# Window attention on one core: the first x in quarters, a key shift from half the keys, and ScalarE evicting at the end

## The chip, the cores and the metric

The kernel runs on one core of a Trainium2 chip. The metric is the device time of one execution in microseconds. A core has five engines that run their own instruction streams and meet at semaphores: TensorE (PE in the profile, its weight loads PEld) multiplies matrices from SBUF into PSUM, VectorE (DVE), ScalarE (ACT) and GpSimd (POOL) work elementwise, SyncE (SP) here only issues DMAs. PSUM has eight banks of 128 x 512 float32. ScalarE and GpSimd can issue DMAs too, in order with their other work.

## The reference: two window attentions and a projection

x is 224 x 224 tokens of 96 channels in bf16. The first 48 channels of q, k, v attend within horizontal bands of 8 rows, the last 48 within vertical bands of 8 columns; each of the 2 x 28 bands has 1792 tokens.

```python
qkv = einsum('bhwc,cd->bhwd', x, wqkv)
ah = softmax(einsum('bqc,bkc->bqk', qh, kh) * scale, axis=-1)   # 28 bands of 1792 tokens, 48 channels
oh = einsum('bqk,bkc->bqc', ah, vh)
...                                                             # the same for the vertical bands
o = concat(oh, ov)
return einsum('bhwc,cd->bhwd', o, wo)
```

A softmax doesn't change when the same vector is taken off every key. The kernel uses that: it shifts the keys by a mean key, to keep the scores small.

## The kernel before

Two bands that lie side by side make a pair; there are 28 pairs P, 14 horizontal and then 14 vertical. Both bands of a pair are worked on at once, in two halves of the 128 partitions. For each pair TensorE makes K, Q (transposed) and V from the turned x; then come 4 chunks of queries (512, 512, 512, 256) against 14 tiles of 128 keys. A score tile covers 2 PSUM banks, 128 x 1024. Most score tiles go to ScalarE, which takes the exponential in one instruction (`emit_qk`, line 867; banks 0, 1 and 2, 3 in turn). The others (246 tiles) get an exponential from a polynomial on VectorE and GpSimd (lines 989 to 1006). PV products (line 723) gather each chunk with its row sum; VectorE evicts it to `OT_sb` (line 884). Horizontal results are turned and kept in `oh_all`. In the vertical phase the two halves are joined, projected with wo (`out_fills`, line 644, called g), evicted to `og` (line 650) and stored. For the last pair the vertical half is projected on its own (`fin_fills`, line 611, called f) and added to `og` with a reciprocal of the sum (lines 618 and 623), two stores' worth of rows at a time.

The whole program is unrolled at build time. `Sched` keeps each engine's list of instructions and derives the semaphore waits from the keys that an instruction reads and writes. The order of the middle comes from `ORDER`, 28 strings, one a pair: `q` is a score tile for ScalarE, `1` to `4` the two score products of a polynomial tile (`3`, `4` and, in capitals, `K`, `G` take two neighbouring banks), `v` a PV product, `k` a K, Q or V product of the next pair, `g` and `f` the output products. A planner in the same file walks the string, keeps a planned time for each engine (`tm`), and uses it to order VectorE's and GpSimd's work and to choose the queue of a store. Constants at the top of the file are its durations; `XR1` and `XR2` are the planned times at which the turned x of pairs 1 and 2 is there. Score products of tiles 1 to `NTWICE` are issued twice.

Ahead of the first string stands a written-out head. The first pair's x comes as two halves for each band, four DMAs, on SP's and ScalarE's queues, then wqkv on SP's; behind these SP blocks, loads and turns the x of pair 1 (lines 291 and 408). TensorE spins on a tile of zeros (`spin`, line 372) until x is there, then transposes it: 8 groups of 4 transposes (`t_lead`, line 745), each group evicted to `xT_sb` by VectorE (line 757) or ScalarE (line 761) with a running sum into `xs_sb`. From all 8 sums a small product (`KB`, line 767) makes the shift `kb_sb` (line 771). Q[0] and K[0] are the first 512 queries and keys; Q[0] is evicted by ScalarE (line 547), K[0] by VectorE with the shift added (line 778), its first 128 keys apart from the rest. Spinning products fill TensorE's planned idle time, in `lead_pe` ahead of each product, and after K[0]'s eviction up to its planned end. `emit` writes every engine's list in that order, so an instruction that waits holds back all that stands behind it on its engine.

At the end `store` gives each finished piece of output to SP's, ScalarE's or GpSimd's queue by planned times.

Of the kernel before, what the change touches and what calls it, by code (L numbers as in the profile page):

```python
# [32 lines left out]
D_ST, D_SW, D_TAIL = 1.0, 0.60, 1.0  # L33
XR1, XR2, TURN = 19.5, 43.0, 4.5
# [5 lines left out]
NTWICE = 11  # L40
# [5 lines left out]
    "kkqqkkq3q3q3qkqkqkqkq1q1qvvq4qkvqkv4qkqvv1qkvqvqvvq4vqkvvqkvq1vqvvq1vkqvkq4vqkvq1vqv2qvkqkqvkq2vvq3qvvvqvkq2vqvvkq",  # L46
    "1qvvvqvq2vvq1qvvqvvq3vvqvvqvkqkvqvKqvvq4qvkvq2qvvq2vqv1qvvqvqv1qvvvq4qvkvq3qvkq2vqv2qvq3vqkvqvvqkq4vqvvq4vqkvq3vqkvvqk",
    "v2qvqv1qvvvvq1qvvvvqvq3vvqvq3kqqvvqvkq4vkqq2vkqv1qkvqvvq4qvkvq3qkvqvkq2qvvq4vqkvq1vvq2qvvkq2qvv1qvvqvvqkvqvvkq1vqv2qvvq",
    "1vq2qvvq1vvqvqvvvqv1qvq1vvqvqvq4qkvq1vqvvqvq2vqv1qvv4qkqvv1qvqvkq2vqkvvq2vkqvkq3vqkqvvvqv1qvq4vqkq3vqkvq4vqvkvq4vqkvq2vk",
    "qvq1vvqvvqv2qvq1vq2qvvvqv2qvvq1qvvvqvvq1qvvqvkvqvkq1qvkqvkvq4vqvvq1qv2qkvqkv1qvvqkvqq2vqkvq1qkvvq2qvvvq1qkkqvvq2vkqvv1",  # L50
    "qvqvvqv2qvvq1vvqvv1qvvqvqv2qq4vqvkq1vqvvvqvq1vqkvkqkvvq2kqv3qkvqv4qvvqkq1vqvvvqkqvv4qvqkv2qvvq2vqv1qvq4vqvvqkvkvq1qkvvq2v",
    "vq1qvvqvvq1vvqvq1vqvvqvv3qvvqvvqvkq2qv1qvqkv2qkvqvq2vvq1qkvvvq2kqq4vqvkq1vvqkqvvq4qkvqv1qvq4vkqvq3vkqvvq3qkvqvvqvvkvq",
    "2qvv1qvvq2vq3qvvqvvqvvq1vqvvvqkqvkvq1qvvkqv2qkvqv2qkvvq1vqv4qvkqvvq2vq4qvvkq1qvkvqvvqv2qvvq2qvv3qvkqv1qvvqkvq4vqvkvq4qvvvkq1",
    "qvvqvvq2vvqvvq1vq2qvvvq1qvvqvq1vkqvvqvkqvkqv2qkvqv2qkq1vqvvq2vqv2qvkvqkq1vqv1qvqvvvqv1qkqvvvq1qkvq2qvkqv2qvvvq1kqvvqk",
    "vqvvq2vvq4qvvvvq1vqvvq4qvkq1qvvqvvvq2vqv1qvvqvkqvkqvvvq2q1qvvq1vvqkvq2vkqv3qkvqvvqvqkq4vqkq3vqvvq4vqkvqk2qvvq1vqvvkq2qkv",
    "vq1vvqvqvvvqv2qvvq1vqvkqkvkqv4qvqvk1qkqvvqv2qvq1vkqvqvvvqv4qvqkq3vqkvq3vqvvq4vqkvq2vqv1qvvqkqvvvqv3qkvqv2qvq1vkqvq2vqv2",
    "qvv1qvqvvvqvv2qvq1vvq1qvvqv1qvqvvq3qvvqvkkqkvq4qkvqv4qkvqv2qvvqv2qvvq3vqvkq1qvvqvkq4qvkqv1qvvvq2qkvqv1qvv2qvkqvkvq2qvk",
# [117 lines left out]
def bass_standalone__window_attn_cswin__vision_kernel(  # L175
# [28 lines left out]
    with es:  # L204
# [1107 lines left out]
        def do_fill(c):  # L1312
# [28 lines left out]
            if g == ("Q", 0, NCH - 1):  # L1341
                turn_x(2)
# [109 lines left out]
```

## Time and profile before

| | us |
|---|---|
| three runs | 1055.43, 1056.22, 1056.88 |
| median of them | 1056.22 |
| the profiled execution | 1057.54 |
| its span, first to last instruction | 1055.7 |
| ScalarE busy in the span | 1041.8 |
| TensorE, VectorE, GpSimd busy | 1027.3, 1014.0, 985.1 |

In a row of the profile a group has its line, engine, operation, the tile written and the tiles read, shapes, the count, the busy time and the mean of one in ns, and then the idle time of the engine ahead of it with what ended it. In a row of the order of time the first number is the start in us from the span's start, the second the length of the merged group; a group's members can overlap, as matmuls do. A row of stages has the stretch, its length, the busy time with the count, the granted TensorE clock, the share of DMA and GB/s.

### The profile page before, as it was taken

To read this page: it belongs to the slowest core of one execution; us is meant where nothing else is said; L and a number is where in the kernel's file an instruction comes from. 1 tells how busy PE (TensorE), PEld (TensorE's weight loads), DVE (VectorE), ACT (ScalarE), POOL (GpSimd) and SP (SyncE) were. 2 spreads that over 40 slices of the span, in tenths; PEclk is the share of its full clock that TensorE was granted. 3 is DMA by queue.
4 is the path that set the end of the run, shared out by engine and by line. 5 is a ranking of instruction groups with operands and counts; after the bars stand their busy time and mean duration, and the time that the engine had idled before them with its cause. 6 is when DMAs were issued, how large, how long until landed. Compare 5 with 4: busy or idle time off the path is not lost.

```text
span 1055.7 us, 32757 instructions
## 1 busy us (share of the span) xinstructions
PE 1027.3 (97%) x13456; PEld 385.9 (37%) x13456; DVE 1014.0 (96%) x1748; ACT 1041.8 (99%) x1137; POOL 985.1 (93%) x654
## 2 busy tenths in 40 slices
PE   9999999999999999999999999999999999999998
PEld 4333333333333333333333433434333333333343
DVE  7989999999999999999999999999999999999998
ACT  7999999999999999999999999999999999999997
POOL 7999999999988998999999999988999999999997
PEclk9999999999999999999999999999999999999999
DMA  9867527654752854222176545537634553674352
GB/s 191 171 133 140 102 51 145 112 96 89 141 94 56 143 104 74 36 59 55 30 77 92 81 91 101 92 52 109 96 64 82 88 91 67 101 100 52 66 75 69
DMA packets 413079, 96.84 MB, mean 92 GB/s; under 512 B 403648, under 2 KB 410016, under 8 KB 412928
## 3 DMA queue, kind: packets, MB, share of 16 engines
q1 hardware_dynamic: 412080, 93.66, 51.8%
q8 instruction: 105, 1.72, 0.7%
q0 software_dynamic: 448, 0.69, 0.2%
q10 hardware_dynamic: 400, 0.39, 0.1%
q14 instruction: 46, 0.38, 0.1%
HBM read 28.31 MB, written 28.21 MB: 54 GB/s over the span
## 4 chain that ended last, share of the span: by engine, by line
PE 54%; ACT 22%; DVE 10%; POOL 7%; issue 6%; DMA 0%; ACTq 0%; POOLq 0%; DVEq 0%
ACT PT L867 22%; PE ps L723 20%; PE ps L697 20%; PE ps L710 7%; DVE PT L994 3%; POOL PT L1002 3%; PE ps L530 3%; DVE qb L989 3%; POOL PT L1005 2%; PE ps L575 1%; POOL PT L1006 1%; PE ps L644 1%; DVE PT L991 1%; DVE og L650 1%; DVE V_sb L582 1%
## 5 line engine op out<-in xcount | busy, mean ns | idle before, releaser
L867 ACT ACTIVATE PT<-ps 128x1024 bf16<-128x1024 f32 x1126 | 1037.2, 1080 | 4.1 <-PE ps L697 2.9
L1002 POOL TENSOR_TENSOR PT<-PT 128x1024 f16<-128x1024 f16 x246 | 461.8, 1894 | 20.3 <-DVE PT L991 11.3
L697 PE MATMUL ps<-QT_sb,KT_sb 49*64 49x512 bf16 (+1 forms) x5332 | 461.6, 362 | 15.9 <-ACT PT L867 9.7
L723 PE MATMUL ps<-PT,V_sb 128*49 128x512 bf16 (+1 forms) x3136 | 464.4, 361 | 0.0
L994 DVE SCALAR_TENSOR_TENSOR PT<-ps,PT 128x512 uint16<-128x512 f32 (+1 forms) x405 | 312.4, 799 | 15.7 <-PE ps L710 6.8
L989 DVE TENSOR_SCALAR qb<-ps 128x512 f16<-128x512 int16 (+1 forms) x421 | 313.7, 775 | 11.9 <-PE ps L710 7.8
L1005 POOL TENSOR_TENSOR PT<-qb 128x1024 f16<-128x1024 f16 x150 | 283.2, 1894 | 22.9 <-DVE qb L989 10.8
L697 PEld LDWEIGHTS ps<-QT_sb,KT_sb 49*64 49x64 bf16 x5332 | 135.4, 104 | 308.3 <-ACT PT L867 284.2
L723 PEld LDWEIGHTS ps<-PT,V_sb 128*49 128x49 bf16 x3136 | 134.2, 103 | 205.7 <-issue 173.5
L710 PE MATMUL ps<-QT_sb,KT_sb 50*64 50x512 bf16 (+1 forms) x1968 | 196.6, 390 | 5.3 <-DVE PT L994 1.2
L1006 POOL TENSOR_SCALAR PT<-PT 128x1024 f16<-128x1024 f16 x150 | 156.9, 1046 | 12.8
L991 DVE SCALAR_TENSOR_TENSOR PT<-ps,qb 128x512 f16<-128x512 int16 (+1 forms) x172 | 123.0, 743 | 0.2
L710 PEld LDWEIGHTS ps<-QT_sb,KT_sb 50*64 50x64 bf16 (+1 forms) x1968 | 55.8, 103 | 76.3 <-DVE PT L994 22.9
L884 DVE CAST OT_sb<-ps 113x512 bf16<-113x512 f32 x112 | 68.9, 615 | 0.5 <-PE ps L723 0.4
L544 DVE CAST QT_sb<-ps 128x512 bf16<-128x512 f32 (+1 forms) x111 | 67.0, 614 | 1.7 <-PE ps L530 1.0
L535 DVE TENSOR_SCALAR_CACHE_REDUCE KT_sb<-ps 128x512 bf16<-128x512 f32 x106 | 63.8, 617 | 1.3 <-PE ps L530 0.8
L650 DVE CAST og<-ps 128x480 bf16<-128x480 f32 x84 | 51.4, 617 | 1.4 <-PE ps L644 0.7
L582 DVE CAST V_sb<-ps 128x480 bf16<-128x480 f32 (+1 forms) x84 | 51.3, 616 | 0.4 <-PE ps L575 0.4
L530 PE MATMUL ps<-xT_sb,w_sb 97*64 97x512 bf16 x224 | 41.9, 371 | 0.3 <-DVE qb L989 0.2
L530 PE MATMUL ps<-xT_sb,wq_sb 97*64 97x512 bf16 x224 | 40.8, 367 | 0.1
L575 PEld LDWEIGHTS ps<-w_sb,xT_sb 96*64 96x64 bf16 x1568 | 33.5, 112 | 16.1 <-issue 7.1
L575 PE MATMUL ps<-w_sb,xT_sb 96*64 96x48 bf16 x1568 | 39.1, 190 | 0.0
(66 smaller groups left out, 248.6 us busy)
## 6 DMA issues: line engine op xcount, KB each, us to landing
xT_sb<-xt_dram SPq DMA_DIRECT2D x28, 336.0 KB, 5.2
xp_dram<-in_x_dram SPq DMA_DIRECT2D x26, 336.0 KB
oc_all<-xp_dram SPq DMA_DIRECT2D x26, 336.0 KB, 3.6
xt_dram<-xT_sb SPq DMA_DIRECT2D x26, 336.0 KB, 6.5
out_dram<-og SPq DMA_DIRECT2D x181, 48.0 KB, 2.0
oh_all<-ohn SPq DMA_DIRECT2D x52, 84.0 KB, 2.8
stg<-oh_all SPq DMA_DIRECT2D x13, 336.0 KB, 6.0
xt_dram<-xT_sb SPq DMA_DIRECT2D x4, 168.0 KB, 4.6
```

The lines of the kernel that those rows point to most:

```text
L530: ins = e.matmul(bk[64 * w:64 * w + 64, 0:qs], lhsT=lw, rhs=xT_sb[b][0:C + 1, w, q0:q0 + qs], start=True, stop=True)
L575: ins = e.matmul(bk[64 * h:64 * h + 64, j * C2:(j + 1) * C2], lhsT=xT_sb[b][0:C, w, t0:t0 + 64], rhs=w_sb[0:C, wblk(P, "v"), 0:C2], start= ...
L697: ins = e.matmul(bank(SETS[s] + w)[64 * kh:64 * kh + 64, i * t["qs"]:(i + 1) * t["qs"]], lhsT=KT_sb[b][64 * w:64 * w + CA, kt * 128 + 64 * ...
L710: ins = e.matmul(bank(bp[w])[64 * kh:64 * kh + 64, 0:512], lhsT=KT_sb[b][64 * w:64 * w + nr, kt * 128 + 64 * kh:kt * 128 + 64 * kh + 64], ...
L723: ins = e.matmul(bank(pb)[64 * w:64 * w + CA, 0:t["qs"]], lhsT=V_sb[b][:, w, kt, :], rhs=PT[slot][:, ca:ca + t["qs"]], start=st and i == 0 ...
L867: S.commit("act", 0.0, D_ACT, None, lambda e, s=s, slot=slot: e.activation(PT[slot][:], ps[:, 512 * SETS[s]:512 * SETS[s] + 1024], ACTF.Ex ...
L989: fn, reads, writes = lambda e: e.tensor_scalar(q, l, m, a, ALU.mult, ALU.add), bk, qk
L991: fn, reads, writes = lambda e: e.scalar_tensor_tensor(y.bitcast(FP16), l, -RA * 2.0 ** 16, q, ALU.add, ALU.mult), bk + qk, ptk
L994: fn, reads, writes = lambda e: e.scalar_tensor_tensor(y.bitcast(U16), f, 128.0, y.bitcast(FP16), ALU.mult, ALU.add), bk + ptk, ptk
L1002: square = ("pool", D_SQ, lambda e: e.tensor_tensor(y, y, y, ALU.mult), yk + ["pser"], yk)
L1005: return [("pool", D_SQ, lambda e: e.tensor_tensor(y, q, q, ALU.mult), qk, yk), ("pool", D_AF, lambda e: e.tensor_scalar(y, y, -(QS * (RB ...
L1006: ("pool", D_AF, lambda e: e.tensor_scalar(y, y, -(QS * (RB + RA) / 2) ** 2, 1.0, ALU.add, ALU.mult), yk + ["pser"], yk),
```

## The change

Five things change together.

- The first x is loaded as eight quarters in place of four halves: for each half and band one quarter on SP's queue and one on ScalarE's. wqkv keeps its place as SP's third DMA. Each group of transposes waits for its own quarter.
- The key shift is made from the sums of the first half alone, four sums in place of eight, with the factor doubled. The evictions of the second half take no sum.
- In the head the last band's second half (two groups of transposes) moves behind Q[0], KB and K[0]; KB moves ahead of K[0]; the spinning products at the head's end go. The new order begins with two score tiles, where the old one began with two K products. Score tiles are issued twice from tile 3 on, before from tile 1; the planner counts more for products while TensorE is planned to be slow.
- From the point where all score tiles are issued, ScalarE evicts the g outputs, and it evicts the last PV chunk. The planned price of a store's issue on SP or ScalarE at the end falls from 1.0 to 0.60, and a store goes to ScalarE's queue only once all PV chunks are closed.
- All 28 strings of `ORDER` are new, and the planner's start times with them.

```diff
-D_ST, D_SW, D_TAIL = 1.0, 0.60, 1.0
-XR1, XR2, TURN = 19.5, 43.0, 4.5
+D_ST, D_SW, D_END = 1.0, 0.60, 0.60
+XR1, XR2, TURN = 20.05, 43.5, 4.5
...
-NTWICE = 11
+NTW0, NTWICE = 3, 11
+CT = 9.5
...
-    "kkqqkkq3q3q3qkqkqkqkq1q1qvvq4qkvqkv4qkqvv1qkvqvqvvq4vqkvvqkvq1vqvvq1vkqvkq4vqkvq1vqv2qvkqkqvkq2vvq3qvvvqvkq2vqvvkq",
+    "qqkkqkkq1qkq3qkqkk3q1qqvq1qkqvv2qvqkvkvq2qkvqkvq3qvkvqvqvkq2kvq1qvkqkq1qvvvqkqvkq1vvq2qvvvq4qvkvq4vqkvq3vqvvvq4qkvvvq1",
...
-    "qvvv1qvvq2vqv1qvvqvvvqgvqv1qvgqgvvq1qvvvgq2qvvq2vqv1qvvvqvvqvq4vqgvq4vqvgvq3fqvvvq4vfqvvq3vqvvqvvqvgq4vfqvvq2vfqvqgvgqffqvvvfqfqfvvfqfvvvgvvfff",
+    "qvv1qvvq1qvvvqvvqv1qgvqv2qvvvq1vqv2qvvq2vqv1qvvqgvvqvqvgqv1qvvfqv2qvvq2vvq2qvvvffqvqv3qvvfqvvqvvq4vfqvvq2vqvffqvvvfqgqvvfqfvgqvgvvffvgff",
...
-        xs_sb = sb("xs_sb", [C, 2, 4], BF16)
-        kbj = sb("kbj", [128, 4], FP32)
+        xs_sb = sb("xs_sb", [C, 2, 2], BF16)
+        kbj = sb("kbj", [128, 2], FP32)
...
+        FQ = FTH // 2
         for hf in range(2):
-            for w, q in ((0, "sp"), (1, "actq")):
-                dma(q, [], [("x", w, hf)], x0_sb[:, w, hf * FTH:(hf + 1) * FTH, :],
-                    x_lead[w][:, hf * FTH * C:(hf + 1) * FTH * C], f"x{w}{hf}", land=3.4 + 1.0 * hf + 0.3 * w)
-        dma("sp", [], ["wst"], wst[:, :], wqkv, "w0", land=5.2)
+            for w in range(2):
+                for h2, q in ((0, "sp"), (1, "actq")):
+                    k0 = hf * FTH + h2 * FQ
+                    dma(q, [], [("x", w, hf, h2)], x0_sb[:, w, k0:k0 + FQ, :],
+                        x_lead[w][:, k0 * C:(k0 + FQ) * C], f"x{w}{hf}{h2}", land=3.2 + 1.9 * hf + 0.4 * w + 0.2 * h2)
+            if hf == 0:
+                dma("sp", [], ["wst"], wst[:, :], wqkv, "w0", land=4.8)
...
+                def da(e, bk, k0=k0, n=n):
+                    return e.activation(rows[:, k0:k0 + n, :], bk[:, 0:n * C].rearrange("p (s c) -> p s c", s=n), ACTF.Copy)
...
             def d(e, bk):
                 dst, src = views(bk)
+                if hf:
+                    return e.tensor_scalar(dst, src, 1.0, None, ALU.mult)
                 return e.tensor_scalar(dst, src, 1.0, None, ALU.mult, ALU.add, accum_out=acc)
...
-            return e.tensor_scalar(kbj[:, :], bk[:, 0:4], -alpha / NTOK, None, ALU.mult, ALU.add, accum_out=kb_sb[:, :])
+            return e.tensor_scalar(kbj[:, :], bk[:, 0:2], -2.0 * alpha / NTOK, None, ALU.mult, ALU.add, accum_out=kb_sb[:, :])
...
-        for w, hf, bs in ((0, 0, (6, 7)), (1, 0, (2, 3)), (0, 1, (6, 7)), (1, 1, (2, 3))):
+        for w, hf, bs in ((0, 0, (6, 7)), (1, 0, (2, 3)), (0, 1, (6, 7))):
             for h2 in range(2):
                 f = t_lead(w, hf, h2)
                 lead_pe(f, bs[h2])
                 lead_ev(f, bs[h2], 0, h2 == 1)
         flags.add(("QB", 0))
         lead_pe(Q[0], 5)
+        lead_pe(KB, 0)
         lead_pe(K[0], 4)
         lead_ev(Q[0], 5, 0, True)
-        lead_pe(KB, 0)
         lead_ev(KB, 0)
         lead_ev(K[0], 4, 0)
         lead_ev(K[0], 4, 1)
-        spin(S.done[("dve", S.cnt["dve"] - 1)])
-        spin(S.done[("dve", S.cnt["dve"] - 1)], 128)
+        for h2 in range(2):
+            f = t_lead(1, 1, h2)
+            lead_pe(f, 6 + h2)
+            lead_ev(f, 6 + h2, 0, h2 == 0)
...
                     if ia[0] >= len(act_seq):
+                        d_t = D_END
+                    if pv_open[0] >= len(pv_chunks):
                         tm["aq"] = max(tm["aq"], tm["act"])
...
+                if (P, c) == (NP - 1, NCH - 1):
+                    tm["act"] = max(tm["act"], st + L_PV) + 0.41
...
+                    S.commit("act", 0.0, 0.41, 0.51, lambda e, b0=acc[0]: e.activation(
+                        OT_sb[P % 2][0:64 + CA, q0:q0 + qs], bank(b0)[0:64 + CA, 0:qs], ACTF.Copy),
+                        [("bank", acc[0])], [("OT", P % 2, c)])
...
+            if c == "g" and ia[0] >= len(act_seq):
+                z = f["chain"][0]
+                tm["act"] = max(tm["act"], st + d + L_FILL) + z[6]
+                done = tm["act"] + 0.1
+                S.commit("act", 0.0, z[6], z[6] + 0.1, lambda e, fn=z[4], bk=bank(b[0]): fn(e, bk), [("bank", b[0])] + z[2], z[3])
+                store(z, done)
+                release(b[0], done)
+                return
```

More of the change, by code (lines that the diff above doesn't have):

```diff
@@ L263, in bass_standalone__window_attn_cswin__vision_kernel @@
             for w in range(2):
-                SEMS[f"x{b}{w}"] = sem(f"s_x{b}{w}")
+                for z in range(2):
+                    SEMS[f"x{b}{w}{z}"] = sem(f"s_x{b}{w}{z}")
                 SEMS[f"xp{b}{w}"] = sem(f"s_xp{b}{w}")
@@ L747, in t_lead @@
             n = FTH * TH
[L748 removed]
+            acc = xs_sb[0:C, w, h2:h2 + 1]
             def views(bk):
@@ L1232, in do_q @@
             st = pe_start("A", r)
-            tw = D_MM if 1 <= ia[0] <= NTWICE else 0
+            tw = D_MM if NTW0 <= ia[0] <= NTWICE else 0
+            if st < CT:
+                tw = 2 * tw + D_MM
             tm["pe"] = st + D_MM + tw
@@ L1337, in do_fill @@
             st = pe_start(f["mode"], max(r, t))
+            if c == "k" and P == 0 and st < CT:
+                d *= 2
             tm["pe"] = st + d
```

93 lines of the change are left out of this document (52 added, 41 removed).

## The prediction

> **What bounds the kernel now.** I read the page first: its line of engine times, then its costliest groups.
>
> ```profile
> span 1055.7 us, 32757 instructions
> PE 1027.3 (97%) x13456; PEld 385.9 (37%) x13456; DVE 1014.0 (96%) x1748; ACT 1041.8 (99%) x1137; POOL 985.1 (93%) x654
> L867 ACT ACTIVATE PT<-ps 128x1024 bf16<-128x1024 f32 x1126 | 1037.2, 1080 | 4.1 <-PE ps L697 2.9
> ```
>
> ScalarE is 99% busy, nearly all of it in 1126 exponentials of line 867, which the change leaves in number and shape. So I cut the span at the first and the last of them (busy time by stages, line 867 alone), and looked at ScalarE's order of time at the start.
>
> ```profile
> 0.00:10.72 10.72, 0.00 (x0) 1.00 0.75 198
> 10.72:1049.82 1039.10, 1037.20 (x1126) 1.00 0.53 91
> 1049.82:1055.71 5.89, 0.00 (x0) 0.93 0.26 77
> ...
> 10.72 5.60 ACT L867 ACTIVATE PT<-ps 128x1024 bf16<-128x1024 f32 x6 [2.26 <-PE ps L697]
> ```
>
> Three stages: a head of 10.72 us without an exponential, 1039.10 us of them, a tail of 5.89 us. The last row gives the step between two that are fed in time: (5.60 - 1.08)/5 = 0.904 us, with 1.08 the mean of one. At that step 1126 would take 1125 x 0.904 + 1.08 = 1018.1 us; 21.0 us of the middle are exponentials that start late by fractions of a microsecond. The change touches all three: it may shorten head and tail, and it rewrites the whole order that feeds the middle.
>
> **The head.** The chain of work before the first exponential, from the order of time, and who lands when:
>
> ```profile
> 0.75 0.92 ACTq L291 DMA_DIRECT2D oh_all<-in_x_dram  x2
> 1.70 1.28 ACT L330 ACT_TABLE_LOAD   x1 [1.70 <-PEq L1437]
> 4.04 3.22 PE L745 MATMUL ps<-ident,oh_all 112*96 112x112 bf16 x32 [0.37 <-DMA oh_all<-in_x_dram]
> L745 PE MATMUL ps<-ident,oh_all x32: 300/301/329, 4.0 to 7.0; 112*96 112x112 bf16 x32
> 5.05 0.54 ACT L761 ACTIVATE xT_sb<-ps 96x448 bf16<-96x448 bf16 x1 [1.85 <-PE ps L745]
> 5.97 0.59 POOL L339 COPY wq_sb<-wst 96x96 bf16<-96x96 bf16 x2
> 7.19 0.64 PE L530 MATMUL ps<-xT_sb,wq_sb 97*64 97x512 bf16 x2
> 7.62 0.64 PE L530 MATMUL ps<-xT_sb,w_sb 97*64 97x512 bf16 x2
> 7.87 0.60 ACT L547 ACTIVATE QT_sb<-ps 128x512 bf16<-128x512 f32 x1
> 8.07 0.29 PE L767 MATMUL ps<-xs_sb,w_sb 96*64 96x4 bf16 x2
> 8.22 0.62 PE L372 MATMUL ps<-warm 128*64 128x512 bf16 x1
> 8.44 0.16 DVE L771 TENSOR_SCALAR_CACHE_REDUCE kbj<-ps 128x4 f32<-128x4 f32 x1 [0.89 <-PE ps L372]
> 8.64 0.88 DVE L778 TENSOR_SCALAR KT_sb<-ps,kb_sb 128x128 bf16<-128x128 f32 x2
> 9.06 0.31 PE L372 MATMUL ps<-warm 128*64 128x128 bf16 x1
> 9.16 1.06 PE L530 MATMUL ps<-xT_sb,w_sb 97*64 97x512 bf16 x2
> 10.15 0.94 PE L697 MATMUL ps<-QT_sb,KT_sb 49*64 49x512 bf16 x12
> ```
>
> x lands at 4.04; 32 transposes, Q0, K0 and the shift follow on TensorE; then spinning products (line 372), K1 and K2 (9.16), and only then, at 10.15, the first scores, 0.57 us before the exponential. The change does three things here.
>
> First load: quarters instead of halves. How fast x moves is a row of the DMA view for 2.5 to 3.5 us:
>
> ```profile
> DMA packets 264, 0.36 MB, mean 356 GB/s; under 512 B 32, under 2 KB 264, under 8 KB 264
> ```
>
> The first transposes wait for 2 x 168 KB that share this rate, 0.97 us; with quarters for 0.48 us of it, if half a packet takes half the time, and for as long as now, if a packet costs the same at any size. Ends: 0.48 and 0 us sooner, and the second halves up to 0.5 us later. I take 0.3, nearer the byte rate: start at 3.74. [...] Behind the two added issues of each queue stand: on ScalarE the table load, 2 x 0.46 later, ending near 3.9; ScalarE idles 1.85 us before its first eviction (5.05, in future about 4.75), so it is covered, and would cost up to 0.9 else. On SP wqkv keeps its third place, now behind 168 KB instead of 336, and the next pair's blocking, loading and turning come about 0.9 us later. Its turned x is issued from 9.67 and first used at 23.43:
>
> ```profile
> 9.67 5.07 SPq L408 DMA_TRANSPOSE xT_sb<-oc_all  x2
> ...
> DMA to landing us min/median/max: 5.3/5.3/5.4
> ...
> 23.43 0.23 PE L504 MATMUL ps<-ident,wq_sb 96*64 96x96 bf16 x2 [0.22 <-DVE PT L994]
> ```
>
> Two turns share the 5.07 us of issue, so the second lands before 14.74 + 5.4 = 20.1 (and after 15.0); 0.9 later, and with the use 2 us sooner, it is 21.0 against 21.4 at the very worst. Nothing, with a stall of at most 1 us if a load in front of it is slow.
>
> Then the order. The starts of 32 transposes lie 31 steps apart, (7.0 - 4.04)/31 = 0.095 us each, 0.38 for four. Six groups of four instead of eight stand before Q0, with three short spins among them (128 columns, a quarter of the 0.43 that 512 take from 7.19 to 7.62): 3.74 + 6 x 0.38 + 0.3 = 6.3. Q0 and K0 take 0.43 each, the shift 0.15 between them (8.07 to the next product at 8.22): K0 issued at 6.88, TensorE free at 7.31; the last two transpose groups 0.76: 8.07. The spins at 8.1 to 9.2 are removed and K1, K2 go behind two score tiles, so the first scores start here if their inputs are there. VectorE: K0's product ends 6.88 + 0.64 = 7.52, the first 128 keys' eviction (0.88 for two) near 7.9. ScalarE: QT at 6.3 + 0.64 + 0.60, by 7.6, then the moved eviction of a transpose, 7.95 + 0.54 = 8.5: it stands ahead of the first exponential, which waits for it and is not delayed by it, since the scores end at 8.07 + 0.6. First exponential at about 8.7, **2.0 us sooner**. Ends: 1.3 (quarters late) and 2.4.
>
> What is late next is the clock. Products of 512 columns took, by line 530 at 7 to 10.3 us and line 697 at 12 to 15:
>
> ```profile
> L530 PE MATMUL ps<-xT_sb,w_sb x6: 634/634/636, 7.6 to 9.6; 97*64 97x512 bf16 x6
> L697 PE MATMUL ps<-QT_sb,KT_sb x32: 376/388/400, 11.8 to 14.8; 49*64 49x512 bf16 x32
> ...
> 12.71 0.63 PE L697 MATMUL ps<-QT_sb,KT_sb 49*64 49x512 bf16 x8
> ```
>
> The clock column reads 1.00 in both stretches, but TensorE runs half as fast, 0.43 a step against 0.63 - 0.39 = 0.24 (eight in two groups, 12.71), until some time after 10, when the first scores stand; I take 10.4, 3.2 us after the unbroken run of products began at 7.19. Now the kernel's first scores fall into the slow time. Up to the third tile that fits the 0.904 step. From the fourth on scores are issued twice (0.86 slow), and a V product or an extra score tile of 0.43 stands between two: 1.29 against 0.904, 0.4 us lost per exponential. If 3.2 us count from 6.3, full speed comes at 9.5, before the fourth tile (11.1): 0.1. If they count from 8.07, at 11.3: 0.5. If a further 2.5 us pass: 1.8. I take **0.5 us lost**. [...]
>
> **The tail.** The order of time after the last exponential, by engine:
>
> ```profile
> 1048.75 1.06 ACT L867 ACTIVATE PT<-ps 128x1024 bf16<-128x1024 f32 x1
> 1049.81 0.44 DVE L650 CAST og<-ps 128x288 bf16<-128x288 f32 x1
> 1050.31 0.42 DVE L884 CAST OT_sb<-ps 113x256 bf16<-113x256 f32 x1
> 1050.79 0.29 PE L611 MATMUL ps<-wov,OT_sb 49*64 49x97 bf16 x8 [0.32 <-DVE OT_sb L884]
> 1051.20 0.30 DVE L623 SCALAR_TENSOR_TENSOR og<-ps,rc,og 128x96 bf16<-128x96 f32 x1
> 1051.41 0.16 DVE L618 RECIPROCAL rc<-ps 128x2 f32<-128x2 f32 x1
> 1051.49 0.97 DVE L623 SCALAR_TENSOR_TENSOR og<-ps,rc,og 128x96 bf16<-128x96 f32 x4
> 1052.53 1.09 POOL L291 DMA_DIRECT2D out_dram<-og  x2 [0.19 <-DVE og L623]
> ...
> DMA to landing us min/median/max: 1.8/2.0/2.3
> ```
>
> The last OT eviction moves to ScalarE: 0.41 by the plan for VectorE's 0.42, no gain in itself. The output evictions go there too, behind it on an engine without exponentials by then, and VectorE loses 0.44 us and one earlier sum (0.30) from its last run: 0.3 us sooner, unless the last sums wait for ScalarE's second eviction, which ends some 0.9 us behind the last product, before the sums start. The last two stores now stand in one queue, POOL's, 1.09 us together; SP's and ScalarE's price in the plan falls from 1.0 to 0.6, so they go to two queues: one issue, 0.55, off the end, less the up to 0.5 by which those land later (1.8 to 2.3). I take 0.3 for that. **Tail 0.6 us shorter**; ends 0.1 and 0.9.
>
> **The middle.** The order lists give TensorE's items; between two scores (q) stand up to five others. Counted in the two lists: three or more items between scores 289 times before (250 of three, 38 of four, 1 of five), 305 after (262, 39, 4). A score and three items are four steps of 0.24, 0.96 us, over the 0.904, so these are where scores come late. If all 21.0 us of lateness sat there it would be 0.073 each, 16 more 1.2 us; if none did, 0; the few of five cost most, and there are three more. I take **1.0 us lost**. As every row of the list differs, the lateness may scatter by 1.5 us either way about that.
>
> **Sum.** -2.0 + 0.5 - 0.6 + 1.0 = -1.1 us. The profiled execution took 1057.54 us, 1.84 outside its span, and stands 1.32 over the median of the three runs, 1056.22. I put the sum on the median: **1055.1 us**, 0.1% less. A difference under 0.2%, 2.1 us, is about what a measurement of this kernel can't tell from no change.
>
> **The rivals.** (a) The middle costs nothing or gains, and the clock rises early: -2.0 - 0.6 + 0.1 with a middle of -0.3, -2.8: 1053.4 us. For it: head and tail are worked from single rows, and the middle's count is a weak guide. Against: it needs two costs to vanish. Chance 0.30.
>
> (b) The quarters come no sooner and the second ones 0.4 us later: a head gain of 1.4 in place of 2.0, 1055.7 us. For it: twice the packets at one rate. Against: first transposes need half the bytes. Chance 0.09.
>
> (c) TensorE stays slow to about 13.8, three or four exponentials lose 0.43 each beyond the 0.5: 1.3 us more, 1056.4 us. For it: transposes interrupt the run of products at 7.3 to 8.1. Against: the products are nearly unbroken from 6.3. Chance 0.13. [...]
>
> (d) Slower: the new list feeds the exponentials worse. Place: scores behind three or more items, in all 28 pairs; price: lateness of 21.0 us grows. Head, clock and tail leave 1056.22 - 2.1 = 1054.1, so it decides from 4.2 us more lateness on, a fifth: 1058.3. At 5 us more it is 1059.1 us. For it: no row of the old list stands, and the old places say nothing of the new. Against: only 6% more places of the long kind. Chance 0.10.
>
> **The numbers.** The forecast has 0.38, with (b) and (c) 0.60 for within 0.2%; (a) 0.30 faster; (d) 0.10 slower. The forecast's own range is 1054.1 to 1056.5; the one given reaches to (a)'s gain with a better middle, 1052.4, and towards (d), 1057.8.
>
> **What would show it.** Right: first transpose near 3.7, first exponential near 8.7, products at 634 ns until 10 to 11.5, last stores on two queues, 5.3 us behind the last exponential; the middle longer than 1039.1 by 0 to 3 us. Wrong: a first exponential behind 9.4, a wait of TensorE for x between transposes, scores 0.4 us late beyond the sixth exponential, or a middle of over 1043.

## The result: 15% slower, and what the profile after shows

The changed kernel takes 1215.1 us in the median (six executions, 1208.0 to 1219.5), the kernel before 1056.0 us beside it (six, 1055.4 to 1056.9). The ratio is 1.1506, 95% interval 1.1469 to 1.1544. The forecast was 1055.1 us, so 160 us are to be explained. The profiled execution took 1213.5 us.

From the page of the changed kernel:

```profile
span 1211.7 us, 32739 instructions
PE 1080.8 (89%) x13448; PEld 392.9 (32%) x13448; DVE 1017.4 (84%) x1739; ACT 1052.2 (87%) x1138; POOL 983.7 (81%) x650
...
PEclk9897999889799889989999999798999889798999
...
L882 ACT ACTIVATE PT<-ps 128x1024 bf16<-128x1024 f32 x1126 | 1046.8, 1071 | 152.3 <-PE ps L706 128.2
...
L536 PE MATMUL ps<-xT_sb,wq_sb 97*64 97x512 bf16 x224 | 43.2, 380 | 105.8 <-DMA xT_sb<-xt_dram 58.7
```

ScalarE does nearly the same work as before (1052.2 us busy against 1041.8, again 1126 exponentials), but it sat idle 152.3 us ahead of the exponentials, line 882 now, where it was 4.1. They waited for scores. TensorE itself is busy 53.5 us longer, and its clock row has many slices of 7 and 8. The last row is the odd one: ahead of the Q products (`wq_sb`; K products read `w_sb`) TensorE sat idle 105.8 us, waiting for DMAs into `xT_sb`. The same group before the change, and then the part of it in the changed kernel that has 256 columns:

```profile
L530 PE MATMUL ps<-xT_sb,wq_sb 97*64 97x512 bf16 x224 | 40.8, 367 | 0.1
...
L536 PE MATMUL ps<-xT_sb,wq_sb 97*64 97x256 bf16 x56 | 9.8, 341 | 101.8 <-DMA xT_sb<-xt_dram 58.7 <-DMA xT_sb<-oc_all 43.1
```

A Q product of 256 columns is the fourth and last chunk of a pair, and nearly all of the waiting is ahead of these. The three stages, cut at the exponentials as in the prediction:

```profile
0.00:7.79 7.79, 0.00 (x0) 1.00 0.65 181
7.79:1206.78 1198.99, 1046.81 (x1126) 0.92 0.44 79
1206.78:1211.73 4.95, 0.00 (x0) 0.72 0.48 129
```

Head and tail came out shorter, as forecast: 7.79 against 10.72 and 4.95 against 5.89. All the loss is in the middle, 1199.0 against 1039.1. The view of waits of the changed kernel (total us, times, longest) says who waits for whom there:

```profile
ACT PT L882 <- PE ps L706: 128.2, 79, 14.8
DVE QT_sb L550 <- PE ps L536: 102.9, 19, 13.3
...
PE ps L536 <- DMA xT_sb<-xt_dram: 58.7, 9, 9.3
PE ps L536 <- DMA xT_sb<-oc_all: 47.0, 8, 13.8
```

Line 550 evicts Q products, so it is a Q product each time. The kernel before has no wait of TensorE for `xT_sb` in that view. The longest case, in the order of time (SyncE's queue and TensorE):

```profile
44.41 2.76 SPq L293 DMA_DIRECT2D xt_dram<-xT_sb  x1
...
44.88 0.41 PE L706 MATMUL ps<-QT_sb,KT_sb 49*64 49x512 bf16 x4
...
47.22 3.39 SPq L293 DMA_DIRECT2D xp_dram<-in_x_dram  x2
...
50.65 0.55 SPq L293 DMA_DIRECT2D wo<-in_wo_dram  x1
51.26 0.87 SPq L293 DMA_DIRECT2D wov<-in_wo_dram  x2
52.17 1.33 SPq L293 DMA_DIRECT2D wov<-one_sb  x2
...
53.61 3.14 SPq L414 DMA_TRANSPOSE xT_sb<-oc_all  x2
...
59.11 0.43 PE L536 MATMUL ps<-xT_sb,wq_sb 97*64 97x256 bf16 x2 [13.82 <-DMA xT_sb<-oc_all]
...
60.74 0.64 PE L706 MATMUL ps<-QT_sb,KT_sb 49*64 49x512 bf16 x4
```

TensorE stops at 45.3 and stands still for 13.82 us in front of a Q product of 256 columns, a last chunk. It waits for a turned x that SyncE starts only at 53.61, behind a store, a blocking and the loads of wo. That x cannot be the product's own: the pair's K and first Q products were made from their x long before.

The code says whose x it is. `xT_sb` has two buffers, so pair P and pair P + 2 share one. At the first score tile of a pair, `do_q` calls `queue_prep`, which commits the refill of that pair's buffer with the x of the pair two further on (`turn_x`, later `plan_x`). Instructions that are committed behind it see the new contents. In the old order every Q product of a pair stands ahead of the pair's first `q`. In the new one 20 do not: the last chunk's product of the 19 pairs 1, 2, 5 to 7, 9 to 14, 18, 19 and 22 to 27, and one more of pair 5, stand one or two `q` behind it. For pairs 26 and 27 there is no pair two further on and so no refill, and their late products, at 1132.21 and 1169.34, wait for nothing. The other 18 read the refilled buffer: Q of those queries is made from the x of the pair two further on, which is also a wrong result. They make 17 waits, since the two of pair 5 share one, and 17 is what the last two rows of the view of waits count. The order can be read off the strings. A pair's share of `q` is 41 for pair 0, and the old first string has 41; the new first string has 43, the last 39, and all between are out of step by two. The new first string ends in

```
q4qkvvvq1
```

and its 42nd `q`, the second from its end, is pair 1's first score tile; the `k` behind it is pair 1's last Q product.

What follows the waits costs time too. Busy time by stretches (PE, PEld, DVE, ACT, POOL, then the granted clock, DMA share and GB/s):

```profile
45.00:59.00 14.00, 0.28 (x4) 0.00 (x0) 1.23 (x1) 1.68 (x2) 12.34 (x23) 0.62 0.89 186
59.00:65.50 6.50, 6.39 (x40) 1.74 (x40) 2.91 (x5) 3.06 (x4) 1.07 (x1) 0.50 1.04 179
66.00:80.00 14.00, 13.69 (x156) 4.75 (x152) 12.26 (x22) 13.76 (x16) 7.04 (x5) 1.00 0.36 86
```

After the wait TensorE is full (6.39 of 6.50 us), but at half clock, and ScalarE gets work for 3.06 us of the 6.5. From 66 on the clock is back and ScalarE is full again. In the clock record 16 stretches at half clock lie between the head and the tail, 188 us together, some of it inside the waits; only the wait of 2.12 us at 613.02 has none behind it.

A ledger of the middle, from the starts of the 1126 exponentials in order of time, each distance less a step of 0.908 us: 18 of them come more than 1.5 us late, 115.8 us together, and 17 of these 18 are one behind each of the 17 waits; 67 more come 0.2 to 1.5 us late inside a stretch at half clock or within 2 us behind it, 44.8 us. That is 160.6 us, and the middle grew by 159.9. What is left, about 16 us, is what the kernel before has in all (16.5).

### The profile page after: what moved, and what is told of

It is laid out like the page before. It is cut to its first block, busy times and chain, and to the rows that moved or that the text cites. A ratio compares the mean times of both kernels' runs of the same rounds, so it can differ in the third digit from the quotient of the medians.

```text
span 1211.7 us, 32739 instructions
## 1 busy us (share of the span) xinstructions
PE 1080.8 (89%) x13448; PEld 392.9 (32%) x13448; DVE 1017.4 (84%) x1739; ACT 1052.2 (87%) x1138; POOL 983.7 (81%) x650
## 4 chain that ended last, share of the span: by engine, by line
PE 52%; ACT 18%; DMA 7%; DVE 7%; POOL 6%; issue 5%; SPq 4%; ACTq 0%; DVEq 0%; POOLq 0%
PE ps L732 21%; PE ps L706 19%; ACT PT L882 18%; PE ps L719 7%; SPq L293 4%; DMA xT_sb<-xt_dram 4%; DMA xT_sb<-oc_all 3%; PE ps L536 3%; DVE qb L1009 3%; POOL PT L1022 2%; POOL PT L1025 2%; DVE PT L1014 1%; PE ps L581 1%; PE ps L650 1%; POOL PT L1026 1%
## 5 line engine op out<-in xcount | busy, mean ns | idle before, releaser
L882 ACT ACTIVATE PT<-ps 128x1024 bf16<-128x1024 f32 x1126 | 1046.8, 1071 | 152.3 <-PE ps L706 128.2
L706 PE MATMUL ps<-QT_sb,KT_sb 49*64 49x512 bf16 (+1 forms) x5324 | 479.9, 377 | 14.6 <-ACT PT L882 9.6
L732 PE MATMUL ps<-PT,V_sb 128*49 128x512 bf16 (+1 forms) x3136 | 492.4, 382 | 0.4 <-DVE KT_sb L939 0.2
L1009 DVE TENSOR_SCALAR qb<-ps 128x512 f16<-128x512 int16 (+1 forms) x424 | 314.8, 771 | 41.7 <-PE ps L719 37.8
L706 PEld LDWEIGHTS ps<-QT_sb,KT_sb 49*64 49x64 bf16 x5324 | 138.3, 105 | 310.5 <-ACT PT L882 253.4
L732 PEld LDWEIGHTS ps<-PT,V_sb 128*49 128x49 bf16 x3136 | 141.0, 106 | 232.1 <-issue 190.9
L719 PE MATMUL ps<-QT_sb,KT_sb 50*64 50x512 bf16 (+1 forms) x1968 | 206.2, 409 | 4.2 <-DVE PT L1014 1.1
L1026 POOL TENSOR_SCALAR PT<-PT 128x1024 f16<-128x1024 f16 x150 | 156.5, 1043 | 12.7
L536 PE MATMUL ps<-xT_sb,wq_sb 97*64 97x512 bf16 x224 | 43.2, 380 | 105.8 <-DMA xT_sb<-xt_dram 58.7
L899 DVE CAST OT_sb<-ps 113x512 bf16<-113x512 f32 x111 | 68.7, 618 | 8.8 <-PE ps L732 8.4
L536 PEld LDWEIGHTS ps<-xT_sb,wq_sb 97*64 97x64 bf16 x224 | 13.2, 110 | 121.7 <-issue 92.7
L986 POOL TENSOR_TENSOR stg<-OT_tr,rn 128x768 bf16<-128x768 bf16 (+1 forms) x26 | 34.1, 1312 | 9.7 <-PE ps L732 5.7
```

The lines of the kernel that those rows point to most:

```text
L536: ins = e.matmul(bk[64 * w:64 * w + 64, 0:qs], lhsT=lw, rhs=xT_sb[b][0:C + 1, w, q0:q0 + qs], start=True, stop=True)
L706: ins = e.matmul(bank(SETS[s] + w)[64 * kh:64 * kh + 64, i * t["qs"]:(i + 1) * t["qs"]], lhsT=KT_sb[b][64 * w:64 * w + CA, kt * 128 + 64 * ...
L719: ins = e.matmul(bank(bp[w])[64 * kh:64 * kh + 64, 0:512], lhsT=KT_sb[b][64 * w:64 * w + nr, kt * 128 + 64 * kh:kt * 128 + 64 * kh + 64], ...
L732: ins = e.matmul(bank(pb)[64 * w:64 * w + CA, 0:t["qs"]], lhsT=V_sb[b][:, w, kt, :], rhs=PT[slot][:, ca:ca + t["qs"]], start=st and i == 0 ...
L882: S.commit("act", 0.0, D_ACT, None, lambda e, s=s, slot=slot: e.activation(PT[slot][:], ps[:, 512 * SETS[s]:512 * SETS[s] + 1024], ACTF.Ex ...
L899: S.commit("dve", 0.0, 0.6, 0.75, lambda e: e.tensor_copy(OT_sb[P % 2][0:64 + CA, q0:q0 + qs], bank(pb)[0:64 + CA, 0:qs]), [("bank", pb)], ...
```

## The experiments

**Do the late products make the loss?** Theory: the late Q products, through the refill, are the loss. The expectations count 20 waits, one for each late product; the traces have 17, as said above. Rival 1 is that the quarters hold up SP's queue; rival 2 is that the new order feeds the exponentials worse throughout, as rival (d) of the prediction has it. Two kernels take the dependence away in different manners, and a third gives it to the old order.

The first pulls each late product ahead of its pair's first score tile.

```diff
+        owed = 0
         for c in "".join(ORDER):
+            while c == "q" and begun and act_seq[ia[0]]["P"] not in begun and prep_q:
+                do_fill("k")
+                owed += 1
+            if c == "k" and owed:
+                owed -= 1
+                continue
```

> The changed kernel, but every Q product that stands behind the first score tile of its own pair in the new order (20 of them, in 19 pairs) is issued just ahead of that tile; nothing else is moved. Theory: each of these 20 waits for the refill of the x buffer that the first tile of the pair has queued, TensorE stands idle behind it, and the clock falls. Then the time is that of my blind sum, 1052 to 1057 us, with no wait of TensorE for x and no slow stretch of the clock between 15 and 1050 us. Rival 1, the quarters hold up SP's queue and every turned x is late: the waits stay, over 1150. Rival 2, the new order is uneven as a whole or too thin at the start to hold the clock: over 1150 too.

Measured: 1070.1 us (six executions, 1069.8 to 1070.4 and one of 1080.8), ratio 1.0147 (1.0119 to 1.0176). No product behind the head waits for x, and the clock record stays at full speed from 6.34 us to 1067.89. So 145 of the 160 us are gone. The forecast for this run was missed: its middle is 1055.4, 16.3 over that of before, and about half of the extra shows at the handovers. Where products were pulled up in front of a pair's first score, the exponentials come up to 1.0 us late (at 194.2, 268.5, 455.4 and others): the first six exponentials of each of these 19 pairs come 10.3 us late all together, and 2.1 in the kernel before. Where the other half lies was not traced.

The second leaves the order as it is and queues the refill only once the last Q product of the pair has been issued.

```diff
+        held = []
+        def refill():
+            P = held[0]
+            if any(f["gives"][:2] == ("Q", P - 1) for f in prep_q):
+                return
+            held.pop(0)
...
         def queue_prep(P):
...
-            if 2 <= P < NPH - 1:
-                turn_x(P + 1)
...
+            held.append(P)
```

> The changed kernel with its order of scores and products untouched; instead the DMAs that refill the x buffer of the pair just begun are queued only when the last Q product of that pair has been issued. The late products then read their own pair's x again (in the changed kernel they read the x of the pair two further on). Theory: what costs is only the dependence on the refill, so 1052 to 1060 us. Rival 2, the place of the products in TensorE's order costs by itself: over 1150. Rival 1: over 1150.

Measured: 1054.7 us (ten executions: six from 1054.3 to 1054.8, four from 1065.1 to 1065.4), ratio 1.0028 (0.9999 to 1.0057). From its trace, the three stages, the stretch that stood still in the changed kernel, and the group that waited:

```profile
0.00:7.99 7.99, 0.00 (x0) 1.00 0.63 179
7.99:1047.83 1039.84, 1037.45 (x1126) 1.00 0.52 91
1047.83:1052.78 4.94, 0.00 (x0) 1.00 0.48 129
```

```profile
45.00:59.00 14.00, 13.80 (x152) 4.93 (x152) 12.22 (x18) 14.00 (x17) 12.75 (x24) 1.00 0.86 182
```

```profile
L536 PE MATMUL ps<-xT_sb,wq_sb 97*64 97x512 bf16 x224 | 41.2, 364 | 0.4 <-DVE QT_sb L550 0.2 <-DVE wq_sb L567 0.2
```

The same items in the same order, and 105.8 us of idle time are 0.4. The middle is 1039.84, 0.75 us over before. That settles the main question: this order as an order costs next to nothing, what it does to the refill costs 160 us. The four executions near 1065 are a matter of their own, taken up below.

The third is the kernel before, with the last Q product of those 19 pairs held back to just behind the pair's first score tile.

```diff
+        late, due = {1, 2, 5, 6, 7, 9, 10, 11, 12, 13, 14, 18, 19, 22, 23, 24, 25, 26, 27}, False
         for c in "".join(ORDER):
+            if c == "k" and prep_q[0]["gives"][0] == "Q" and prep_q[0]["gives"][2] == NCH - 1 and prep_q[0]["gives"][1] in late:
+                due = True
+                continue
             if c == "q":
                 do_q()
+                if due and act_seq[ia[0] - 1]["P"] == prep_q[0]["gives"][1]:
+                    do_fill("k")
+                    due = False
```

> The kernel before with one thing changed: in the same 19 pairs the last Q product (256 queries) is moved behind the pair's first score tile; head, tail, loads and everything else as before. These products read the x of the pair two further on. Theory: 19 waits of 2 to 14 us and slow clock behind most: 1150 to 1230 us. Rivals 1 and 2, which blame the quarters or the new order: 1055 to 1060 us.

Measured: 1210.7 us in one execution. Its waits (PEld is TensorE's loading of weights):

```profile
ACT PT L867 <- PE ps L697: 123.4, 94, 12.5
...
PE ps L530 <- DMA xT_sb<-xt_dram: 46.5, 8, 11.8
PEld ps L530 <- DMA xT_sb<-xt_dram: 34.6, 4, 12.3
PE ps L530 <- DMA xT_sb<-oc_all: 33.5, 7, 11.8
```

The old order, with nothing else of the change, shows the same kind of waits and of half-clock stretches (16, 201 us together) and nearly the same time. It has no quarters and no new order, so both rivals fall, and the theory is shown from both sides: taking the dependence away takes the loss away, and adding it to the old kernel adds the loss.

**What does one late product cost?** Same edit with one pair in the set, pair 7 first (`late = {7}`).

> The kernel before with the last Q product of one pair, pair 7, behind that pair's first score tile (it reads the x of pair 9). Theory: one wait of TensorE of 4 to 8 us near 310 us, one slow stretch of the clock of about 10 us behind it, and in total 6 to 12 us: 1062 to 1068 us. If the wait alone counts and the slow clock is made good by the slack of TensorE: 1060 to 1063. Rivals 1 and 2: 1055 to 1057.

Measured: 1058.0 us (ten executions, 1057.3 to 1061.7), ratio 1.0019 (1.0010 to 1.0028). The expectation was too high. Then pair 1 (`late = {1}`), the longest wait:

> The kernel before, with the last Q product of pair 1 alone issued behind that pair's first score tile, so that it waits for the refill of its buffer and takes the x of pair 3 (that part of the result is changed). Pair 7's product alone waited 2.52 us without a fall of the clock and cost 1.6 us. Pair 1's waited 11.82 us in the kernel with 19 late products and 13.82 us in the changed kernel. If the price of a late product is the wait plus a stretch at half clock behind it, this one alone gives 12 us of wait and, at half clock for some 10 to 16 us behind it, 3 to 9 us more: 1069 to 1078 us. If the wait alone is lost, 1066 to 1069 us. If the exponentials draw on tiles that stand ready, under 1063 us.

Measured: 1070.8 us (four executions, 1069.0 to 1072.0), ratio 1.0136 (1.0121 to 1.0151). The two waiting products, of pair 7 and of pair 1:

```profile
269.70 0.30 PE L530 MATMUL ps<-xT_sb,wq_sb 97*64 97x256 bf16 x2 [2.52 <-DMA xT_sb<-oc_all]
```

```profile
57.72 0.42 PE L530 MATMUL ps<-xT_sb,wq_sb 97*64 97x256 bf16 x2 [11.71 <-DMA xT_sb<-oc_all]
```

and the stretches around the second:

```profile
45.60:57.70 12.10, 0.41 (x4) 0.12 (x5) 2.37 (x4) 1.78 (x2) 10.89 (x22) 0.63 0.82 179
57.70:69.30 11.60, 11.58 (x78) 3.47 (x80) 5.35 (x8) 6.24 (x7) 4.17 (x3) 0.50 0.86 172
70.00:80.00 10.00, 9.91 (x106) 3.22 (x102) 7.76 (x16) 9.92 (x12) 4.83 (x3) 1.00 0.25 48
```

Pair 7: 2.52 us of wait, no fall of the clock in the traced execution, one exponential 2.86 us late. The three executions of that kernel with a mean clock under 0.998 took 1059.0 to 1061.7, which fits a fall of the clock that adds a few us, but they were not traced. Pair 1: 11.71 of wait, then 11.6 us at half clock in which ScalarE has work for 6.24; the middle is 15.7 us longer than before's. The price of this late product is its wait and about a third more. In the changed kernel, where most waits are shorter, 105.7 us of waits cost 160, half more.

**Head and tail by themselves.** The kernel before with the new head, the old order kept but for its first seven items (`kkqqkkq` becomes `qqkkqkk`), and the old tail:

```diff
-    "kkqqkkq3q3q3qkqkqkqkq1q1qvvq4qkvqkv4qkqvv1qkvqvqvvq4vqkvvqkvq1vqvvq1vkqvkq4vqkvq1vqv2qvkqkqvkq2vvq3qvvvqvkq2vqvvkq",
+    "qqkkqkk3q3q3qkqkqkqkq1q1qvvq4qkvqkv4qkqvv1qkvqvqvvq4vqkvvqkvq1vqvvq1vkqvkq4vqkvq1vqv2qvkqkqvkq2vvq3qvvvqvkq2vqvvkq",
```

> The kernel before with the new head alone: quarters, key shift from the first half's sums, the last two transpose groups behind K0, no spins at the head's end; the old order of all pairs but for its first seven items, which become qqkkqkk in place of kkqqkkq; the old tail. By the trace of the kernel with its refills held back the first exponential starts at 8.0 instead of 10.7 us: 2.7 us less than a run of the kernel before whose TensorE is slow to 10.4, 1.1 less than one whose clock rose early (first exponential at 9.1). So 1054.3 to 1055.3. If the head is also what gives the second group of times near 1065, some of its runs show it.

Measured: 1060.8 us (three executions from 1060.7 to 1060.9, one of 1080.9), ratio 1.0044 (1.0027 to 1.0060). The first exponential stands at 7.91, but the middle is 1045.29, 6.2 longer: 4 us of it are lost in the first 75 exponentials, 0.4 to 0.7 us late at 11.3, 14.7, 23.4, 29.4 and 36.6. The clock rose at 5.79, so it is not the half clock: the old list does not fit the new start. The forecast, a gain, was missed.

The kernel before with the new tail alone (ScalarE evicting, the lower price of a store, the last OT on ScalarE):

```diff
+                if (P, c) == (NP - 1, NCH - 1):
...
+                    S.commit("act", 0.0, 0.41, 0.51, lambda e, b0=acc[0]: e.activation(
...
+            if c == "g" and ia[0] >= len(act_seq):
...
+                S.commit("act", 0.0, z[6], z[6] + 0.1, lambda e, fn=z[4], bk=bank(b[0]): fn(e, bk), [("bank", b[0])] + z[2], z[3])
```

> The kernel before with the new tail alone: ScalarE evicts the last PV chunk and the output products behind the last score tile, stores go to its queue at the end, price 0.60. In the changed kernel 4.95 us lie behind the last exponential, before 5.90: about 0.9 us less, 1055.0 to 1055.8. With the old order's end (three f last, one g behind the last score) the gain may be less, down to 0.4. If the tail gives the second group of times near 1065, some of its runs show it.

Measured: 1054.7 us (ten executions, 1054.3 to 1056.2), ratio 0.9988 (0.9979 to 0.9997). By its ratio it is the only kernel here that is faster than before, by an amount near the limit of what can be told. Its order of time at the end:

```profile
1048.61 0.46 ACT L652 ACTIVATE og<-ps 128x288 bf16<-128x288 f32 x1
...
1049.35 0.38 ACT L1319 ACTIVATE OT_sb<-ps 113x256 bf16<-113x256 f32 x1 [0.28 <-PE ps L725]
1049.36 1.09 POOL L291 DMA_DIRECT2D out_dram<-og  x2 [0.96 <-ACT og L652]
...
1051.42 0.65 ACTq L291 DMA_DIRECT2D out_dram<-og  x1
```

The evictions are on ScalarE, one store is issued on its queue near the end, and the tail is 5.13 us against 5.89.

Head and tail together on the old order (the first seven items changed as above):

> New head and new tail with the old order (its first seven items changed as in the head run): no product of a pair behind its first score tile, the old middle. Head and tail add: 1.1 to 2.7 and 0.5 to 0.9 less than the kernel before, 1052.8 to 1054.5, and 0.7 under the kernel with its refills held back, whose middle was 0.75 us longer.

Measured: 1059.7 us (ten executions: seven from 1059.4 to 1060.1, three from 1066.0 to 1066.2), ratio 1.0050 (1.0031 to 1.0069). First exponential 7.84, middle 1044.74, tail 5.11: the loss of the new head on the old list, and the gain of the tail. Expected was a gain.

**Halves instead of quarters,** in the kernel with the refill held back:

```diff
-            for w in range(2):
-                for h2, q in ((0, "sp"), (1, "actq")):
-                    k0 = hf * FTH + h2 * FQ
-                    dma(q, [], [("x", w, hf, h2)], x0_sb[:, w, k0:k0 + FQ, :],
-                        x_lead[w][:, k0 * C:(k0 + FQ) * C], f"x{w}{hf}{h2}", land=3.2 + 1.9 * hf + 0.4 * w + 0.2 * h2)
+            for w, q in ((0, "sp"), (1, "actq")):
+                dma(q, [], [("x", w, hf, 0), ("x", w, hf, 1)], x0_sb[:, w, hf * FTH:(hf + 1) * FTH, :],
+                    x_lead[w][:, hf * FTH * C:(hf + 1) * FTH * C], f"x{w}{hf}0", land=3.2 + 1.9 * hf + 0.4 * w)
```

> The kernel with its refills held back, but x loaded as four halves, each on the queue where its band stood, wqkv still behind 168 KB on SP's. My blind step says 0.3 us for the quarters, between 0 and 0.5: first exponential 0.3 us later than 8.0, and 1054.8 to 1055.1 beside 1054.5. If the quarters carry the head's gain, 1 us or more.

Measured: 1065.8 us (four executions, 1063.7 to 1069.8), ratio 1.0085 (1.0068 to 1.0101). TensorE waits for the halves:

```profile
4.29 1.73 PE L752 MATMUL ps<-ident,oh_all 112*96 112x112 bf16 x16 [0.84 <-DMA oh_all<-in_x_dram]
```

With quarters the same transposes start at 3.38. The first exponential is at 9.97, and another 13 us are lost in the first 75 exponentials. My first reading was that the list falls apart when the start is late; the next runs show another cause for the larger part, a late clock. So the time of this run doesn't price the quarters; only its start of the transposes does.

**The group near 1065.** Executions some 6 to 11 us slower, and one 20, appear only in kernels with the new head. Theory: they are made at the start, where TensorE runs at half clock (634 ns for a product of 512 columns at 7.6 to 9.6 us in the kernel before) and score products are issued twice. One kernel drops the doubled products (`NTW0, NTWICE = 3, 2`, the refill held back), and the kernel with the refill held back is run twice more for its trace.

> The changed kernel with its refills held back until the last Q product of the pair has been issued, and with no score product issued twice at the fourth to twelfth tile (those that a tile before 9.5 us doubles in the planner's times are left in the times, so that the order is the same). The same kernel with the doubled products has 6 runs of 10 at 1054.3 to 1054.8 and 4 at 1065.1 to 1065.4. Theory: the second group is made in the first 15 us, where TensorE at half clock can't keep up with doubled products when the clock rises late. By it the doubled products are what costs, and without them no run lies near 1065: all at 1053.5 to 1056. Rival: the doubled products are what brings the clock up; without them it rises later or falls again, and most runs lie at 1060 or above. Second rival: the second group has nothing to do with the start, and about 4 of 10 runs are 10 us slower here too.

> The same text as the kernel with the refills held back, run again for its trace. Four chances in ten for a run near 1065. If it is one, the theory of the start expects the clock to rise later than the 5 to 6 us of the traced run at 1054, and the 10 us lost within the first 75 exponentials (which then take 78 to 82 us in place of 68.8); the rival expects the loss spread over the middle or in one place behind 100 us.

> As the run before it, once more: a run near 1065 with its loss in the first 75 exponentials if the theory of the start holds, or a run near 1054.5 with the first exponential at 8.0 us.

Measured: without doubled products 1061.4 us (six executions, 1057.3 to 1065.6), ratio 1.0049 (1.0031 to 1.0068); in the traced one the clock rose at 5.7, fell again at 12.55 and came back at 33.0. Four of the six have a mean clock of 0.994 or less, which fits a fall in each of them. So the first part of the theory fell and its rival fits: the doubled products are not the fault, and without them the clock did not hold. The two repetitions took 1060.2 and 1064.9 us and were both caught with a trace. TensorE's groups from 20 to 30 us, first of the trace at 1054.6, then of the one at 1064.9:

```profile
L706 PE MATMUL ps<-QT_sb,KT_sb 49*64 49x512 bf16 x44 | 4.5, 398 | 0.5 <-ACT PT L891 0.4
```

```profile
L706 PE MATMUL ps<-QT_sb,KT_sb 49*64 49x512 bf16 x48 | 6.7, 631 | 0.0
```

and all engines in the same 10 us, in the same order:

```profile
20.00:30.00 10.00, 9.41 (x100) 2.92 (x96) 9.38 (x22) 10.00 (x12) 9.84 (x7) 1.00 0.90 152
```

```profile
20.00:30.00 10.00, 10.00 (x74) 2.62 (x68) 6.88 (x10) 7.39 (x8) 9.84 (x7) 1.00 0.99 166
```

In the slower execution a score product still takes 631 ns at 20 to 30 us, TensorE is full with 74 products where it did 100, and ScalarE idles a quarter of the time. (The clock column reads 1.00 since the record of the clock begins with its first change.) In the clock record the first change, the rise, stands at 5.28 us in the execution at 1054.6, at 23.5 in that at 1060.2, at 37.8 in that at 1064.9, and at 50.3 in the traced one with halves. The first 75 exponentials took 68.8, 73.5, 78.5 and 82.1 us. So in the traced executions the group is one and the same program with a clock that rises late; the other slow ones, those of 1080.8 and 1080.9 us among them, have no trace. Why it rises late with the new head is open. With the old head it rose between 4.3 and 10.4 us in all traces, and no execution of the kernel before or of the one with the new tail alone fell into such a group.

## Why the prediction was wrong

**The step that failed** is the one of the middle: "The order lists give TensorE's items", counted by how many stand between two scores, "I take 1.0 us lost". It treated the list as a sequence of durations. An item of the list also fixes what has been committed ahead of it, and a pair's first `q` commits the refill of the buffer that the pair's Q products read. The prediction never asked, for each `k`, on which side of its pair's first `q` it stands, and so put the waits at nothing. The runs showed in their place 17 waits of TensorE for the refill, 105.7 us, and the half clock behind them: 160 us together. The `q` count of the strings, 43 and 39 where 41 belong, would have pointed at it.

Without the dependence the middle is 0.75 us longer than before, near the 1.0 forecast, but that is luck. The count of places with three or more items is 289 before, 290 in the kernel with the new head and the old order, 305 in the new order and 310 in the first repair; the middles are 6.2, 0.75 and 16.3 us longer. The count does not tell them apart.

**Rival (d)** pointed to the right stage and the wrong mechanism: it had lateness of 5 us spread over scores behind three or more items. The loss is 17 waits for DMAs and the half clock behind them. A middle of over 1043 was named as a sign against the forecast, and it showed; a wait of TensorE for x was named for the head alone.

**The head** is 2.0 us sooner by the prediction, ends 1.3 and 2.4. Measured 2.93 in the changed kernel, but part of that is the clock's. Five traces with the old head have the first exponential at 10.72, 10.25, 9.13, 8.76 and 8.75 us with the clock's rise at 10.41, 9.21, 5.66, 4.46 and 4.27. At a like rise, 8.76 (4.46) stands against 7.79 (4.10) and 9.13 (5.66) against 7.84 to 7.91 (5.72 to 5.79): 1.0 to 1.3 us. With a late clock it is 10.72 against 9.27 and 9.07 (the executions at 1060.2 and 1064.9), 1.45 and 1.65. So the prediction's 2.0 was too large, at or under its lower end when the clock comes early. Its order of steps held. One row was misread, without harm: the product at 23.43 reads wq and the identity, and the first that reads the turned x of pair 1 stands at 24.36. Rows of the changed kernel:

```profile
5.56 0.56 PE L754 MATMUL ps<-ident,oh_all 112*96 112x112 bf16 x8 [0.58 <-DMA oh_all<-in_x_dram]
6.06 0.41 PE L536 MATMUL ps<-xT_sb,wq_sb 97*64 97x512 bf16 x2
...
7.33 0.84 PE L706 MATMUL ps<-QT_sb,KT_sb 49*64 49x512 bf16 x8
```

Of the parts, the quarters were mis-sized: 0.3 us forecast, with ends of 0 and 0.48; the first transposes start at 3.38 where they stood at 4.04, 0.66 sooner, and with halves in the same kernel they start at 4.29, 0.91 later. The named sign "a wait of TensorE for x between transposes" also shows, 0.58 us for a second quarter, and did not undo the gain.

**The clock** was put at 0.5 us lost, between 0.1 and 1.8, from one trace in which it rose at 10.4 us, 3.2 us behind the first Q product. That distance did not carry over: in the changed kernel the clock rose at 4.10, ahead of the first Q product at 6.06, when TensorE had done only spinning products (from 1.00) and some of the 16 transposes that start at 3.38. Whether transposes break the run of products for the clock, which rival (c) hung on, no run here shows. Nor does one show the further 2.5 us behind the range's 1.8 and (c)'s 13.8: the first rises that were traced stand at 4.10 to 10.41 us and, the late ones, at 23.5, 37.8 and 50.3. In the traced execution at 1054.6 nothing is lost to the clock (68.8 us for the first 75 exponentials, 68.7 before), in those with a late rise 4.2 us (middle 1044.07, rise at 23.5) to 9.2 us (1049.05, rise at 37.8). The range should have come from several executions; one profile shows one draw.

**The tail** was 0.6 us shorter by the prediction, ends 0.1 and 0.9. Measured 0.94 in the changed kernel (5.89 to 4.95), just past its end, and about 0.8 with the new tail alone on the old order. The two halves of the term were mis-sized in opposite ways. VectorE's last sum ends 2.45 us behind the last exponential where it was 2.65, 0.2 sooner and not 0.3; from there to the end it is 2.50 us where it was 3.25, 0.75 sooner and not 0.3.

**The sum** of the prediction, -1.1 us on 1056.2, is 1055.1; the kernel that differs from the changed one only in when the refill is queued runs in six of its twelve executions at 1054.3 to 1054.8. That it comes so near is in part luck, since the misses cancel: a head of 1.0 to 1.3 us at a like clock for 2.0, against a tail, a clock and a middle that each came out 0.25 to 0.5 us better. The term that was missing was worth 160 us.

## What to carry to other kernels

Where a program is unrolled from an order list, a moved letter moves a commit, so for every buffer that is refilled check that each of its readers still stands ahead of the refill; count the letters that trigger refills against the group sizes. The sign in a profile is a product that waits for a DMA into a tile that it should have had for long. And a stall of TensorE cost more here than its own length, 160 us for 105.7: price it with the slow stretch behind it, and take head times from more than one execution.

## What the runs showed of the hardware

In the changed kernel the clock fell with 16 of the 17 stalls of TensorE for the refill. The stalls of 13.82, 3.84 and 2.58 us (products at 59.11, 102.40 and 393.95) each come with a stretch at half clock (17.07, 13.65 and 10.24 us long), and the one of 2.12 us does not:

```profile
613.02 0.30 PE L536 MATMUL ps<-xT_sb,wq_sb 97*64 97x256 bf16 x2 [2.12 <-DMA xT_sb<-xt_dram]
```

The 2.52 us of pair 7 had none either, while 2.07 us at 216.04 in the kernel with 19 late products had one of 10.2 us. What decides it for stalls this short is not shown. The 16 stretches between head and tail last 3.41 us (one), 6.83 (one), 10.24 (seven), 13.65 (four) and 17.07 (three) in the clock record of the changed kernel, each a whole multiple of the shortest.

I had not expected that full speed can stay away from a full TensorE, as it did in these runs. TensorE was busy in all of the 27.8 us from 10.0 to 37.8 in the execution at 1064.9, and only then did the clock rise. Behind stalls TensorE was full for 11.6 us before the clock came back in pair 1's case above, and for 36.7 us (759.4 to 796.1) in the kernel with 19 late products; ten of these 36.7 us:

```profile
780.00:790.00 10.00, 10.00 (x64) 2.05 (x60) 5.59 (x10) 6.82 (x7) 7.45 (x5) 0.50 0.27 20
```

What brings the clock back is not shown by any run here.
